# Retention and two expert layers on one core: one load task is moved ahead, one expert's row preparation is moved back

## The chip, the cores and the metric

One core of a Trainium2 chip runs the whole program. Times are microseconds of device time for one launch. The kernel before took 1059.43 us in the median of three runs (1049.46 to 1062.60). An execution of its own was profiled and is read below.

## The reference

Three stages, all in float32. The first is causal attention with a decay instead of a softmax; the second and third send each of 4608 tokens of 512 values through one of eight experts (512 to 1024 to 512, with a ReLU).

```python
scores = scale * q @ k.T                     # 8 x 8 heads, 576 x 576, width 64
x = (scores * gamma ** (i - j) * (j <= i)) @ v
x = x.transpose(0, 2, 1, 3).reshape(4608, 512)

logits = x @ w_gate                          # first layer: each token to its best expert
e = argmax(logits); out[t] = softmax(logits)[t, e] * (relu(x[t] @ w1[e]) @ w2[e])

logits = out @ w_gate2                       # second layer: all (token, expert) pairs by falling logit,
                                             # a token to the first expert that has room (576 each)
out2[t] = relu(out[t] @ w1b[e]) @ w2b[e]
```

In the second layer experts fill up one after the other; the kernel looks for them in eight phases, in the order in which they become full.

## The kernel before, in words

**Arithmetic.** Each f32 operand is split into two f16 parts, so a product is three f16 matmuls (high by high, high by low, low by high). Weights come in quarters of 512 KB through three `stage` buffers (`load_half`, L416 to L478): ACT writes the high part (L469), VectorE the low part (L472). The generator gives up control five times: the first turn issues loads 0 and 1, the next four each cast one quarter, the first two of these also issuing loads 2 and 3. Where `behind` is set, each load is pinned behind what SP was given before; casts are pinned likewise on their engines.

**First expert layer** (`moe1`, L988). Eight experts in order of their count, e = 0 to 7. `layer1` makes h for all of an expert's rows: 8 blocks of 24 matmuls into `ph`, which has two PSUM buffers; ACT takes the ReLU (L593), VectorE the rest (L594). `layer2` makes a tile of 128 rows with 24 matmuls of 512 columns; `out_rows` scales it and `second` (L1071) puts it to `X1`, by SP (L1077, the last tiles, 36 to 39 of 40) or by an indirect DMA of POOL (L1088). For e = 6 and e = 7 only `layer1` runs at first; their ten row tiles follow in `rest` (L1218), and the choice for the second layer begins under them.

Other work is hung on step numbers of `layer1`'s 192 matmuls. `prep(e)` (L1014) lists and gathers an expert's rows; each of its further turns normalises a tile of 128 rows (square L517, scaled copy L530, low half L533, all behind each other) and transposes it by DMA on SP (L544). Rows are built in three `xhl` buffers. For e = 6 these turns, which prepare the eighth expert (e = 7), stand at the steps in `N6`. `gate2` (L700) folds the second layer's gate into w2: four pairs of DMA transposes of w2 on SP (L711, two `w2T` buffer pairs) and sixteen small matmuls for each (L718, L719). For e = 6 its turns stand at `G6`: the first two issue pairs 0 and 1, the third uses pair 0 and issues pair 2, the fourth uses pair 1 and issues pair 3, the fifth uses pair 2; the last pair is used at step 24 of e = 7.

**Second expert layer** (`moe2`, L1744). `choose` finds the threshold at which the next expert is full, five rounds of a comparison on VectorE (L1545), a count on PE (L1551), and two small matmuls more (L1559, L1566); its "sum" (L1583) gives the expert's number, and `listed` its rows. All of it is issued piecewise by `during` (L1830): after each matmul the nominal time of its columns at 2.4 GHz is taken off three counters, and what has run out issues its next piece. `tasks` holds the loads and row turns to come, as pairs (first, function), one every 2700 ns (`GAP`) in the first phases. `prepare` (L1810) puts them there: for phase 0 the five turns of w1's `load_half` once the expert is known, for later phases everything once the list is known. `due(True)` runs tasks until none with `first` is left; `due(False)` runs all. w1's tasks and row turns have `first` set, w2's have not.

Phase 0 takes its rows from X1: three gathers before the last tiles are stored (`soon`, from the eighth row tile on), two behind them (`fetched`). PE transposes three of these tiles under the tenth row tile at its steps 12, 16 and 20 (`turned`: L550 on PE, L551 on ACT, L552 on VectorE), the other two at steps 76 and 88 of phase 0's `layer1`. Then `due(False)`, `fetched(0)` and `half(0, 2)` put w2's five tasks on the empty list, and phase 0 begins.

**Order.** PE's instructions, the loads, casts and row preparations named above are pinned to the program's order behind what precedes them on their engine. What is not pinned (the reads of PSUM, the scaling and storing of rows, the gathers) is placed in each engine's queue by a scheduler when the kernel is built. At run time each queue is worked in its order.

Of the kernel before, what the change touches and what calls it, by code (L numbers as in the profile page):

```python
# [36 lines left out]
RANK = (32, 40, 48)  # L37
N1 = (14, 82, 102, 122, 142, 170)
LOGITS = (96, 99, 101, 105, 109)
N6 = (24, 42, 60, 78, 94)  # L40
G6 = (4, 8, 40, 122, 139)
G7 = (30, 36, 70, 106, 140, 170)
R = 5
NONE = -1.0e30
# [658 lines left out]
def gate2(k, w, n):  # L703

    nc = k.nc
    pg = k.fps.tile([128, 8, 16], F32, name="tp")

    def turned(i):
        t = k.fp.tile([128, 2, 8, 128], F16, name="w2T", bufs=2)
        for z, x in enumerate((w.w2h, w.w2l)):  # L710
            pe(k, nc.sync.dma_start(t[:, z], x[:, 2 * i:2 * i + 2, :].rearrange("p f d -> p (f d)"), transpose=True))  # L711
        return t

    def used(i, t):
        for j in range(2):
            f = 2 * i + j
            for c in range(4):
                pe(k, nc.tensor.matmul(pg[:, f, :], t[:, 0, 4 * j + c, :], k.wgl[:, c, :], start=c == 0, stop=False, skip_group_check=True))  # L718
                pe(k, nc.tensor.matmul(pg[:, f, 0:8], t[:, 1, 4 * j + c, :], k.wgl[:, c, 0:8], start=False, stop=c == 3, skip_group_check=True))  # L719

    ts = [turned(0)]
    yield
    ts.append(turned(1))
    yield
    for i in range(4):
        used(i, ts[i])
        if i < 2:
            ts.append(turned(i + 2))
        if i < 3:
            yield  # L730
    f = k.fp.tile([128, 8, 8], F32, name="wgf", bufs=1)
    nc.vector.tensor_reduce(f, pg.rearrange("p s (n e) -> p s e n", n=2), op=OP.add, axis=AX.X)
    g = k.fp.tile([128, 8, 16], F16, name=f"wgh{n}", bufs=1)
    nc.vector.tensor_scalar(g[:, :, 0:8], f, 2.0 ** -7, None, op0=OP.mult)
    nc.vector.scalar_tensor_tensor(g[:, :, 8:16], f, 2.0 ** -7, g[:, :, 0:8], op0=OP.mult, op1=OP.subtract)
    return g
# [251 lines left out]
def moe1(k, X, X1, w1, w2):  # L988
# [110 lines left out]
    for e in range(8):  # L1099
# [24 lines left out]
        elif e < 7:  # L1124
            p1 = ahead
            for i in N6 if e == 6 else N1:
                steps[i] = lambda: next(p1, None)
# [25 lines left out]
        if e > 5:  # L1153
# [5 lines left out]
            gates[e] = gate2(k, w, e)  # L1159
            for i in G6 if e == 6 else G7:  # L1160
                steps[i] = partial(step, e, gates[e])
# [582 lines left out]
def moe2(k, X1, w1, w2, out, rest):  # L1744
# [9 lines left out]
    def side():  # L1754

        with k.tc.high_priority(offset=1000):
            t = next(aside[0], None)
        if t is None:
            aside.pop(0)
            prepare()  # L1760
        state.side = ASIDE.get(t, 0)
# [16 lines left out]
    def choose_on():  # L1778
        with k.tc.high_priority(offset=1000):
            state.left = next(choice, 1e9)  # L1780
        prepare()

    def half(n, i):

        w = weights.setdefault(n, K())
        g = load_half(k, w, (None, w1, w2)[i][ds(ev[n], 1)].rearrange("o d f -> (o d) f"), i, 4, behind=True)
        tasks.extend([(i == 1, lambda: next(g, None))] * 5)

    def soon():

        if 0 not in rows:
            rows[0] = [gather(k, X1[0:128 * (NS - LATE), :], lx[0][:, s:s + 1]) for s in range(SOON)]
            xTs[0] = new_xT(k)
# [16 lines left out]
    def prepare():  # L1810

        n = state.ph + 1
        if n == 0:
            if 0 in ev and 0 not in weights:
                half(0, 1)
        elif n in lx and n not in weights:
            half(n, 1)
            t = tasks[-5:]
            del tasks[-5:]
            r = [(True, partial(turned, n, s)) for s in range(5)]  # L1820
            pair = lambda *fs: (True, lambda: [f() for _, f in fs])
            tasks.extend([(True, partial(fetched, n))] + t[:2] + [pair(*r[:3])] + t[2:3] + [pair(*r[3:])] + t[3:])
            half(n, 2)

    def due(first):

        while tasks and (not first or any(x for x, _ in tasks)):
            tasks.pop(0)[1]()
# [46 lines left out]
    rest(resting)  # L1875
    while not lx:
        choose_on()
    due(False)
    soon()
    fetched(0)  # L1880
    for s in range(len(turns), SOON):
        turned(0, s)
    turns[:] = [partial(turned, 0, s) for s in range(SOON, 5)]
    half(0, 2)
    for ph in range(8):
        while ph and ph not in weights:
            if aside:
                side()
            else:
                choose_on()  # L1890
        due(True)
        state.ph = ph
        prepare()
        w = weights[ph]
        h = during(later(layer1(k, xTs[ph], w, CAP2, spans=None if ph else [[(0, 128 * SOON)], [(128 * SOON, CAP2 - 128 * SOON)]])))
        while not hasattr(w, "whole"):
            tasks.pop(0)[1]()
        for s in range(5) if ph < 7 else (4, 0, 1, 2, 3):
            tail = s == 4
            py = during(layer2(k, h, w, s, tail))  # L1900
            to_out(k, py, scales[ph][s], tail, out, out2)


def program(tc, q, kk, v, wg1, w11, w12, wg2, w21, w22, consts, out, dbg=None):
    nc = tc.nc
    ctx = ExitStack()
    k = K()
    k.pin = False
    setup(k, tc, nc, ctx, consts)
    moe_setup(k, ctx)  # L1910
    X = tc.dram_tile([128 * NT, W], F32, name="Xs")
    X1 = tc.dram_tile([128 * NS, W], F32, name="X1s")
    LG = tc.dram_tile([128 * NS, 8], F32, name="LGsd")
    k.wgl = split_gate(k, wg2, "wg2")
    select_setup(k)
    k.w = {0: K()}
    attention(k, q, kk, v, wg1, consts, X, [(load_half(k, k.w[0], w11[0], 1, 4, steps=False, spread=True), *CAST)], early(k, X))
    open_ffn(k)
    rest = moe1(k, X, X1, w11, w12)
    k.wn, k.xn, k.yn = 8, 9, 0  # L1920
    moe2(k, X1, w21, w22, out, rest)
    k.pin = False
    n = nc.values_load(k.again[0:1, 0:1], min_val=0, max_val=1, skip_runtime_bounds_check_because="0 or 1")
    with tc.For_i(0, n):
        overflow(k, X, X1, LG, w11, w12)
        anew(k, X1, w21, w22, out)
    if dbg:
        dbg(k, X, X1, LG)
    k.fctx.close()
    ctx.close()  # L1930
# [25 lines left out]
```

## Time and profile before

| | before |
|---|---|
| median of three runs | 1059.43 us |
| the three runs | 1049.46, 1059.43, 1062.60 us |
| the profiled execution | 1056.06 us |
| its span, first to last instruction | 1054.2 us |
| mean granted TensorE clock | 0.984 |
| PE, VectorE, ACT, POOL busy | 95%, 58%, 40%, 29% |

The profile shows instructions with their line, engine, operation and tiles. A wait is the idle time of an engine before an instruction, put down to what released it. PE is TensorE's matmuls; SPq and POOLq are the issues of DMAs. The granted clock is a share of 2.4 GHz, and 0.5 is the lower level of 1.2 GHz. In time, the first expert layer's seventh `layer1` runs from 503.94 us, the eighth from 540.5, the ten row tiles from 571 to 631, phase 0 of the second expert layer from 631.28.

### The profile page before, as it was taken

How to read it: one execution, taken by the hardware profiler on the slowest of the kernel's cores; microseconds unless marked ns; L12 is line 12 of the kernel's file. 1: busy time of each engine (PE TensorE's matmuls, PEld its weight loads, DVE VectorE, ACT ScalarE, POOL GpSimd, SP SyncE). 2: the span in 40 equal slices, each digit the busy share in tenths (PEclk: the TensorE clock that was granted, in tenths of full speed). 3: DMA queues.
4: the chain of work that ended last, by engine and by line, in shares of the span. 5: the costliest groups of instructions: out<-in, count | busy, mean ns of one | idle time of the engine just before them, and what ended most of it. 6: DMA issues, size and time to landing. Idle time of an engine off the chain costs nothing.

```text
span 1054.2 us, 23316 instructions
## 1 busy us (share of the span) xinstructions
PE 1003.0 (95%) x9165; PEld 669.1 (63%) x9165; DVE 611.6 (58%) x1648; ACT 426.5 (40%) x810; POOL 307.0 (29%) x542
## 2 busy tenths in 40 slices
PE   6999998889999999999899998999999999999995
PEld 5888887546665757474567445574747474757572
DVE  3556765786766657567443676575648484625230
ACT  2555644464546555455421244233324242323330
POOL 5444454331130303020320231414141413414101
PEclk9999998899999999999999999999999999999998
DMA  9999998597787887779951153758265546746501
GB/s 191 213 238 243 227 241 220 140 249 175 206 227 155 215 183 203 174 199 235 218 87 32 41 158 111 189 170 201 101 126 170 151 140 162 230 128 178 141 27 43
DMA packets 304918, 177.64 MB, mean 169 GB/s; under 512 B 239136, under 2 KB 272416, under 8 KB 304800
## 3 DMA queue, kind: packets, MB, share of 16 engines
q1 hardware_dynamic: 293680, 140.83, 57.7%
q0 software_dynamic: 11120, 35.24, 10.4%
q8 instruction: 74, 1.21, 0.5%
q14 instruction: 44, 0.36, 0.1%
HBM read 116.83 MB, written 31.02 MB: 140 GB/s over the span
## 4 chain that ended last, share of the span: by engine, by line
PE 75%; DMA 9%; DVE 8%; issue 3%; ACT 3%; SPq 1%; POOL 0%; POOLq 0%; ACTq 0%; DVEq 0%
PE py L614 29%; PE ph L588 27%; PE tp L123 7%; PE pO L123 4%; PE pS L123 4%; DMA xg<-Xs,ix 3%; DMA q<-in_q_dram 2%; PE py L610 2%; DMA xT<-xhl 2%; DVE w1l L472 1%; DVE hl L594 1%; DVE w2l L472 1%; DMA stage<-in_moe_w_dram 1%; SPq L123 1%; DVE xhl L533 1%
## 5 line engine op out<-in xcount | busy, mean ns | idle before, releaser
L588 PE MATMUL ph<-xT,w1h 128*128 128x288 f16 (+6 forms) x2048 | 357.4, 290 | 16.7 <-DVE hl L594 6.9
L588 PEld LDWEIGHTS <-w1h 128*128 128x128 f16 x2048 | 196.2, 98 | 77.3 <-issue 21.4
L588 PE MATMUL ph<-xT,w1l 128*128 128x288 f16 (+6 forms) x1024 | 225.9, 290 | 0.0
L614 PE MATMUL py<-w2l,hh 128*128 128x512 f16 x512 | 194.1, 379 | 1.0 <-DVE w2l L472 1.0
L614 PE MATMUL py<-w2h,hh 128*128 128x512 f16 x512 | 194.2, 379 | 0.3 <-ACT w2h L469 0.3
L614 PE MATMUL py<-w2h,hl 128*128 128x512 f16 x512 | 194.2, 379 | 0.0
L614 PEld LDWEIGHTS <-hh 128*128 128x128 f16 x1024 | 98.3, 98 | 109.4 <-issue 1.0
L593 ACT ACTIVATE hh<-ph 128x576 f16<-128x576 f32 (+6 forms) x136 | 80.8, 594 | 169.8 <-PE ph L588 168.2
L594 DVE SCALAR_TENSOR_TENSOR hl<-ph,hh 128x576 f16<-128x576 f32 (+6 forms) x136 | 93.9, 691 | 57.9 <-ACT hh L593 57.3
L588 PEld LDWEIGHTS <-w1l 128*128 128x128 f16 x1024 | 99.9, 98 | 29.0 <-issue 2.6
L472 DVE SCALAR_TENSOR_TENSOR w1l<-stage,w1h 128x1024 f16<-128x1024 f32 x60 | 73.1, 1222 | 41.6 <-ACT w1h L469 40.8
L614 PEld LDWEIGHTS <-hl 128*128 128x128 f16 x512 | 50.0, 98 | 57.0 <-issue 1.3
L472 DVE SCALAR_TENSOR_TENSOR w2l<-stage,w2h 128x1024 f16<-128x1024 f32 x64 | 78.2, 1223 | 11.6 <-ACT w2h L469 11.1
L503 POOL DMA_INDIRECT xg<-X1s,ix x40 | 46.1, 1152 | 108.3 <-DVE ix L658 56.7
L123 DVE TENSOR_TENSOR s<-pS,ct 128x512 f32<-128x512 f32 x72 | 46.4, 686 | 43.2 <-PE pS L123 43.1
L469 ACT ACTIVATE w2h<-stage 128x1024 f16<-128x1024 f32 x64 | 66.9, 1048 | 4.8 <-DMA stage<-in_moe_w_dram 4.8
L469 ACT ACTIVATE w1h<-stage 128x1024 f16<-128x1024 f32 x60 | 62.3, 1047 | 1.6 <-DMA stage<-in_moe_w_dram 1.6
L517 ACT ACTIVATE x1r<-py 128x512 bf16<-128x512 f32 x37 | 22.1, 596 | 96.2 <-PE py L614 64.3
L123 POOL TENSOR_TENSOR xTl<-xT,xTh 128x512 f16<-128x512 f32 x34 | 39.6, 1164 | 64.3 <-ACT xTh L123 64.2
L671 POOL TENSOR_TENSOR x1r<-nm,sc 128x1 f32<-128x1 f32 x34 | 6.4, 190 | 177.2 <-DVE nm L384 174.8
L123 ACT ACTIVATE kT<-tp 128x512 f32<-128x512 f32 x36 | 21.5, 597 | 87.4 <-PE tp L123 87.4
L503 POOL DMA_INDIRECT xg<-Xs,ix x36 | 42.3, 1176 | 43.4 <-DVE ix L658 29.2
(399 smaller groups left out, 1459.8 us busy)
## 6 DMA issues: line engine op xcount, KB each, us to landing
stage<-in_moe_w_dram SPq DMA_DIRECT2D x128, 512.0 KB, 4.6
X1s<-x1r SPq DMA_DIRECT2D x32, 257.0 KB, 3.2
k<-in_k_dram SPq DMA_DIRECT2D x32, 256.0 KB, 5.5
q<-in_q_dram SPq DMA_DIRECT2D x32, 256.0 KB, 5.5
v<-in_v_dram SPq DMA_DIRECT2D x32, 256.0 KB, 5.2
Xs<-xr SPq DMA_DIRECT2D x5, 1028.0 KB, 7.2
Xs<-xr POOLq DMA_DIRECT2D x3, 771.0 KB, 4.4
Xs<-xr POOLq DMA_DIRECT2D x1, 1028.0 KB, 5.6
```

The source lines that it names most:

```text
L123: return lambda *args, **kw: self.tc.keep_in_program_order(f(*args, **kw))
L469: d = nc.scalar.activation(at(h, i), t, AF.Copy, scale=128.0)
L472: d = nc.vector.scalar_tensor_tensor(at(l, i), t, 128.0, at(h, i), op0=OP.mult, op1=OP.subtract)
L503: nc.gpsimd.indirect_dma_start(out=xg[:M], out_offset=None, in_=src, in_offset=bass.IndirectOffsetOnAxis(ap=gidx[:M], axis=0))
L517: d = nc.scalar.activation(q.bitcast(mybir.dt.bfloat16), x, AF.Square, accum_out=sc[:, 0:1])
L533: nc.vector.scalar_tensor_tensor(h[:, 512:1024], x, sc[:, 1:2], h[:, 0:512], op0=OP.mult, op1=OP.subtract)
L588: pe(k, nc.tensor.matmul(ph[:, z, :b], x[:, c, F], xT[:, y + c, a:a + b], start=i == 0, stop=i == 11))
L593: nc.scalar.activation(oh, src, AF.Relu)
L594: nc.vector.scalar_tensor_tensor(ol, src, 0.0, oh, op0=OP.max, op1=OP.subtract)
L610: pe(k, nc.tensor.matmul(py[64 * z:64 * z + 64, 0:256], x[:, f, S], y[:, f, 256 * z:256 * z + 256], start=i == 0, stop=i == 23))
L614: pe(k, nc.tensor.matmul(py, x[:, f, S], y[:, f, :], start=i == 0, stop=i == 23))
L671: nc.gpsimd.tensor_tensor(xr[:, 512:513], n[:, 2:3], sc[:, 0:1], op=OP.mult)
```

## The change

Four edits. The steps in `N6` go from 24 to 94 to 46 to 126; the last three in `G6` go from 40, 122 and 139 to 137, 150 and 170. For phase 0, `prepare` puts w2's five tasks behind w1's as soon as the expert is known, and the call of `half(0, 2)` at the end of the row tiles is gone. `due` ahead of phase 0 runs only as long as a task with `first` is left.

```diff
-N6 = (24, 42, 60, 78, 94)
-G6 = (4, 8, 40, 122, 139)
+N6 = (46, 66, 86, 106, 126)
+G6 = (4, 8, 137, 150, 170)
@@ prepare()
         if n == 0:
             if 0 in ev and 0 not in weights:
                 half(0, 1)
+                half(0, 2)
@@ between rest(resting) and phase 0
-    due(False)
+    due(True)
     soon()
     fetched(0)
     for s in range(len(turns), SOON):
         turned(0, s)
     turns[:] = [partial(turned, 0, s) for s in range(SOON, 5)]
-    half(0, 2)
```

## Rows read from the trace of the kernel before

**Rows 1.** page part 1, busy time of each engine

```profile
PE 1003.0 (95%) x9165; PEld 669.1 (63%) x9165; DVE 611.6 (58%) x1648; ACT 426.5 (40%) x810; POOL 307.0 (29%) x542
```

**Rows 2.** waits of PE, 498 to 545 us: total, times, longest

```profile
PE ph L588 <- DVE sc L534: 3.7, 1, 3.7
PE ph L588 <- DVE hl L594: 2.8, 2, 1.6
```

**Rows 3.** timeline of PE: start, us, engine, line, instructions, [idle before]

```profile
503.94 0.43 PE L588 MATMUL ph<-xT,w1h 128*128 128x320 f16 x2
...
528.57 0.69 PE L588 MATMUL ph<-xT,w1h 128*128 128x320 f16 x2 [3.69 <-DVE sc L534]
...
543.78 0.17 PE L718 MATMUL tp<-wg2s,w2T 128*128 128x16 f16 x1
...
544.19 0.70 PE L588 MATMUL ph<-xT,w1h 128*128 128x320 f16 x4
544.73 0.43 PE L588 MATMUL ph<-xT,w1l 128*128 128x320 f16 x2
```

**Rows 4.** windows: us, PE, PEld, DVE, ACT, POOL busy, PEclk, DMA

```profile
528.57:531.97 3.40, 3.40 (x28) 2.13 (x28) 3.23 (x16) 1.24 (x3) 2.01 (x2) 0.53 0.25 45
...
644.88:647.91 3.03, 3.03 (x11) 1.28 (x12) 2.10 (x6) 1.69 (x3) 1.99 (x8) 0.51 0.36 139
```

**Rows 5.** timeline of ACT in the seventh expert's first layer

```profile
512.26 0.63 ACT L517 ACTIVATE xhl<-xg 128x512 bf16<-128x512 f32 x1 [2.51 <-DMA xg<-Xs,ix]
...
521.99 0.63 ACT L517 ACTIVATE xhl<-xg 128x512 bf16<-128x512 f32 x1 [2.79 <-DMA xT<-xhl]
...
526.35 0.63 ACT L517 ACTIVATE xhl<-xg 128x512 bf16<-128x512 f32 x1 [2.45 <-DMA xT<-xhl]
```

**Rows 6.** timeline of SP in the same layer

```profile
514.48 2.28 SPq L544 DMA_TRANSPOSE xT<-xhl  x1
516.86 2.41 SPq L711 DMA_TRANSPOSE w2T<-w2h  x1
...
521.67 4.27 SPq L544 DMA_TRANSPOSE xT<-xhl  x3
```

**Rows 7.** DMA of tile w2T, 490 to 560 us, from issue to landing

```profile
DMA to landing us min/median/max: 3.1/3.3/5.9
```

**Rows 8.** DMA of tile stage, 600 to 700 us, from issue to landing

```profile
DMA to landing us min/median/max: 3.6/4.2/4.9
```

**Rows 9.** waits of PE, 626 to 664 us

```profile
PE ph L588 <- DVE hl L594: 2.6, 2, 2.5
```

**Rows 10.** timelines of ACT and VectorE, phase 0 of the second layer

```profile
640.49 1.06 ACT L469 ACTIVATE w2h<-stage 128x1024 f16<-128x1024 f32 x1 [1.80 <-DMA stage<-in_moe_w_dram]
...
641.58 2.50 DVE L472 SCALAR_TENSOR_TENSOR w2l<-stage,w2h 128x1024 f16<-128x1024 f32 x2 [1.29 <-ACT w2h L469]
```

**Rows 11.** timeline of SP around the last row stores

```profile
622.69 0.34 SPq L1077 DMA_DIRECT2D X1s<-x1r  x1
...
635.03 0.32 SPq L1077 DMA_DIRECT2D X1s<-x1r  x1
635.56 1.54 SPq L438 DMA_DIRECT2D stage<-in_moe_w_dram  x3
```

**Rows 12.** waits of SP, 600 to 650 us

```profile
SPq L1077 <- POOL x1r L671: 8.7, 2, 5.5
```

**Rows 13.** timeline of POOL under the row tiles

```profile
617.94 1.40 POOL L503 DMA_INDIRECT xg<-X1s,ix  x1 [2.64 <-DVE key L1541]
```

**Rows 14.** timelines of PE and VectorE under the row tiles

```profile
603.29 0.17 PE L1583 MATMUL tp<-s,one_h 128*128 128x8 f16 x1
...
626.54 0.31 PE L1551 MATMUL tp<-ch,cmp 128*128 128x64 f16 x5
...
624.05 0.23 DVE L1569 SCALAR_TENSOR_TENSOR thf<-fstep,bw,tp 128x16 f32<-128x16 f32 x1 [1.76 <-PE tp L1566]
...
624.32 0.85 DVE L1545 TENSOR_TENSOR cmp<-key,thf 128x640 f16<-128x640 f32 x1
```

## The prediction

> **What bounds the kernel now.** I read the page first: TensorE is busy for 1003.0 of 1054.2 us [rows 1]. So a change here pays only what it takes from the idle or half-speed time of PE. The diff touches two stretches: the first layer of the seventh expert (served seventh, e = 6, from 503.94 us) and the border between the two MoE layers (604 to 663 us). For each I asked for PE's waits, then for the timeline of the queue that released them.
>
> In the seventh expert's first layer PE waits 3.7 us once and 2.8 us in two pieces, both times for VectorE [rows 2]; the granted clock then reads 0.53 for 3.40 us, the 1.2 GHz level, after an idle 3.69 us [rows 3, 4]. VectorE is not the cause. ACT works its queue in order, and the squares of the eighth expert's rows (L517) stand in it ahead of the reads of PSUM (L593): the square at 512.26 waited 2.51 us for a gather, those at 521.99 and 526.35 waited 2.79 and 2.45 us for a transposed row to leave its buffer [rows 5]. SP shows why those were late: row 0's transpose at 514.48, then the gate's transposes of w2 (one of the two is shown), and only at 521.67 rows 1 to 3 [rows 6].
>
> At the border PE waits 2.6 us (2.5 and 0.2), again for VectorE [rows 9], and the next 3.03 us have a clock of 0.51 [rows 4]. Here it is the second weights of phase 0: ACT stands 1.80 us for their load, and VectorE's 2.50 us of two low halves (L472) lie ahead of the read that frees PSUM [rows 10]. The loads were issued at 635.56, behind the last row store at 635.03 [rows 11].
>
> **The change, part B (N6, G6): what it removes.** One step is a matmul of 320 columns: four take 0.54 us [rows 3], so 0.136 us. Rows were normalised at steps 24 to 94, now at 46 to 126. Squares of rows 3 and 4 now stand behind the reads of blocks 3 and 4 instead of ahead of block 3's; and with the gate's later turns at 137 and 150, no w2 transpose is left between the rows' transposes. Row 0's was in use from 514.48 to 521.99, 7.5 us; row 1's from 521.67 to 526.35, 4.7 us [rows 5, 6]. From an issue at about 512.5 row 0's buffer is free by 517 to 520. The third square's new place (step 106, PE at about 518.5) and the fourth's (step 126, about 522) then wait for less than the 1.5 us of slack that two PSUM buffers leave. Removed: 3.7 + 2.8 us of waits, and 3.40 us at 0.53, which is 1.6 less what is not matmul there; I take 1.5. Together 8.0 us. Least: the 3.7 and the 1.5 alone, 5.2.
>
> **Part B: what it adds.** No instruction is added. But the gate's third pair of w2 turns now goes out behind row 4's transpose. Row 4 is squared at about 522 and its transpose is out by 526 (row 3 now: squared at 521.99, out by 525.94 [rows 5, 6]). The second w2 transpose starts 1.3 to 2.4 us later [rows 6] and lands 3.3 us after that (3.1 to 5.9) [rows 7]: 530.6 to 531.7, I take 531.5. PE wants it at step 170: 503.94 + 170 x 0.136, plus two gate groups of 0.41 us and five logits groups half as long [rows 3], is 529.0. So PE waits 2.5 us at this new place; bounds 0 (row 4 is early) and 6.0 (landing 5.9 makes 4.5, the clock 1.5 more). I add no clock here, though the 2.5 us at the border were enough for 1.5 us of it [rows 4, 9]. The eighth expert's own first matmul, at about 534.5, finds row 4 landed. Part B: -8.0 + 2.5 = -5.5 us.
>
> **Part A (w2 of phase 0): where its five tasks now stand.** The list grows where the first choice's sum is done, 603.29, six matmuls into the eighth expert's first tile [rows 14]. A task runs every 2700 ns, 13 matmuls of 213 ns. Five tasks of w1, then w2: first two loads behind the 23rd matmul of the third tile (before that tile's own store is issued, behind the second's), first casts on ACT and VectorE behind the 12th of the fourth, the next two at the first and 14th of the fifth, the last cast four matmuls into phase 0. due(True) leaves that last one there.
>
> What holds SP: the second tile's store went only at 622.69. SP waited 5.5 us for POOL's scale of that row (L671) alone [rows 11, 12], and POOL had three gathers ahead of it, the first from 617.94 [rows 13]. The diff does not touch that order. So the loads go out at 622.69 + 0.53 (the distance in [rows 11]) = 623.2, 12 us earlier than now, and land 4.2 us later (3.6 to 4.9) [rows 8]: 627.4. The page "DMA: Bandwidth & Descriptors" of the Trainium skill (section "Anatomy of one DMA") gives 2.0 us plus bytes at 436 GB/s, an estimate of 3.2 us for 512 KB; by it the wait below is 1 us shorter, and the landings here do not show it.
>
> What stands behind the cast: the queues' order is written at build time, and the scheduler took loads as landed too early in the very same pattern now (1.80 us on ACT, [rows 10]). I take it that it puts the first cast on ACT ahead of the fourth tile's square and its low half on VectorE ahead of the choice's next threshold (624.05) [rows 14]. Then VectorE is blocked until 627.4 + 1.06 + 1.25 = 629.8; threshold and comparison took 1.12 us from 624.05 [rows 14]: 630.9. PE's count matmul, now at 626.54, waits **4.4 us** (3.8 to 5.1 by the landings; 0 if the queues are ordered the other way). Behind it ACT and VectorE hold two more casts (1.06 and 1.25 each) ahead of the PSUM copies of phase 0's row turns, which have two buffers: between 0 and 3.3, I take 1.7. A wait over 2.4 us was followed by the 1.2 GHz level both times [rows 3, 4, 9]: 1.5 more. The last cast lies ahead of phase 0's first PSUM read: 0 to 1.2, 0.5. Paid: 8.1 us (0 to 11.1).
>
> What comes back: 2.6 us of waits and half of 3.03 us, 1.5: 4.1 us [rows 4, 9]. Part A: +8.1 - 4.1 = +4.0 us.
>
> **Sum.** -5.5 + 4.0 = -1.5 us. The profiled execution took 1056.06 us (1.9 outside its span), so 1054.5. The median of the three runs is 3.4 higher, their spread 13.1; the forecast lies 4.9 under that median.
>
> **The rivals.** (1) *Both parts pay.* The cast is queued behind the comparison, or the store goes early, so nothing is paid at the border: -5.5 - 4.1 = -9.6, 1046.5. For it: 12 us of earlier issue. Against: [rows 12, 13]. The same page's section "Rules for kernel authors" would have it so: issue the DMA early, compute, wait late. No run here shows it; only half of the rule is met, as the wait comes early too. (2) *The same, and w2's turns land in time*: -8.0 - 4.1 = -12.1, 1044. For it: landings of 3.1 us [rows 7]. Against: they queue behind row 4. (3) *Slower*: the loads land later than 5.7 us after their issue. Gains are 8.0 - 2.5 + 4.1 = 9.6, the price 8.1 at a landing of 4.2; each further us is PE's. At 8.5 us it is +2.8, 1059. For it: gathers of rows run beside these loads, and a transpose took 5.9 [rows 7]. Against: no stage load did over 4.9 [rows 8].
>
> **How the numbers follow.** Forecast 0.45 (alone 1050 to 1058), rival 1 0.25, rival 2 0.1, rival 3 0.2. The range takes all four and the spread of single runs: 1043 to 1063. Two per cent, about what a measurement of this kernel tells from no change, is 21 us; no case reaches it, so same 0.93, faster 0.04, slower 0.03 for orders that shift elsewhere when the queues are laid out anew.
>
> **What would show it.** Right for B: no PE wait over 1 us before step 137 of that layer, clock 1.00 throughout, one wait of 2 to 3 us at the third gate group. Right for A: phase 0's w2 loads at about 623 less B's gain, ACT idle before the first cast, a PE wait of 4 to 5 us before a count matmul in the eighth expert's fourth or fifth tile, and none behind phase 0's fourth block. Wrong: ACT's first cast without idle (rival 1), POOL's scale ahead of the gathers, or PE waiting for the row turns of the eighth expert.

## The result and the profile after

The changed kernel is slower: 1061.8 us against 1055.0 us of before (medians of 20 runs each), a ratio of 1.0062 with a 95% interval of 1.0039 to 1.0085. That is +6.5 us (4.1 to 9.0), where the forecast was -1.5. The profiled execution took 1062.01 us.

The page (part 1) shows that PE's own work did not change, as [rows 1] of before has 1003.0 us; the loss is waiting and half speed:

```profile
span 1060.2 us, 23317 instructions
...
PE 1004.3 (95%) x9165; PEld 668.9 (63%) x9165; DVE 612.8 (58%) x1648; ACT 426.4 (40%) x810; POOL 305.0 (29%) x542
```

**The border between the layers.** PE's waits, 626 to 664 us (total, times, longest), which answer to [rows 9]:

```profile
PE tp L1551 <- DVE nm L382: 5.8, 1, 5.8
PE ph L588 <- DVE hl L594: 1.4, 2, 1.2
```

The old wait has shrunk from 2.6 to 1.4 us, and a new one of 5.8 us stands in the row tiles, at the count matmul. The timeline of SP shows the loads early, at 623.23 instead of 635.56 [rows 11]:

```profile
622.61 0.34 SPq L1077 DMA_DIRECT2D X1s<-x1r  x1
623.23 1.35 SPq L438 DMA_DIRECT2D stage<-in_moe_w_dram  x2
626.20 0.34 SPq L1077 DMA_DIRECT2D X1s<-x1r  x1
626.74 0.37 SPq L438 DMA_DIRECT2D stage<-in_moe_w_dram  x1
634.42 0.34 SPq L1077 DMA_DIRECT2D X1s<-x1r  x1
```

and those of ACT and VectorE (start, us, [idle before and who ended it]) show that their consumers were earlier still:

```profile
620.60 0.69 ACT L669 ACTIVATE x1r<-py,nm 128x512 f16<-128x512 f32 x1 [1.01 <-DVE nm L383]
629.15 1.06 ACT L469 ACTIVATE w2h<-stage 128x1024 f16<-128x1024 f32 x1 [7.87 <-DMA stage<-in_moe_w_dram]
...
630.24 1.23 DVE L472 SCALAR_TENSOR_TENSOR w2l<-stage,w2h 128x1024 f16<-128x1024 f32 x1 [7.92 <-ACT w2h L469]
631.38 0.23 DVE L1569 SCALAR_TENSOR_TENSOR thf<-fstep,bw,tp 128x16 f32<-128x16 f32 x1
631.53 0.15 DVE L1571 TENSOR_TENSOR lof<-bw,tp 128x1 f32<-128x1 f32 x1
631.64 0.82 DVE L1545 TENSOR_TENSOR cmp<-key,thf 128x640 f16<-128x640 f32 x1
```

Both engines stood for 7.9 us at the first cast, each with work behind it that PE needed: the threshold L1569 ran at 631.38, in before at 624.05 [rows 14]. PE resumed at 632.52, and the window behind that (us, PE, PEld, DVE, ACT, POOL busy, PEclk, DMA) shows the 1.2 GHz level for 5.58 us, worth 2.8 us:

```profile
632.52:638.10 5.58, 5.58 (x31) 3.09 (x31) 4.14 (x9) 3.77 (x5) 0.19 (x1) 0.50 0.45 111
```

**The seventh expert's first layer.** PE's waits, 498 to 545 us, which answer to [rows 2]; then ACT's one wait for a transposed row, where [rows 5] has two, and the issue of that row on SP, where [rows 6] has 514.48 and 2.28 us:

```profile
PE ph L588 <- DVE sc L382: 4.3, 1, 4.3
PE tp L719 <- DMA w2T<-w2l: 2.1, 1, 2.1
PE tp L693 <- DMA x1T<-x1r: 2.0, 1, 2.0
```

```profile
507.81 7.67 SPq L544 DMA_TRANSPOSE xT<-xhl  x1
...
521.36 0.63 ACT L517 ACTIVATE xhl<-xg 128x512 bf16<-128x512 f32 x1 [5.90 <-DMA xT<-xhl]
```

The rows' squares did move, and the wait on the row buffer moved with them, in one piece of 5.90 us instead of 2.79 and 2.45. The forecast had it gone. The half-speed stretch came with it (window behind the 4.3 us, 526 to 532 us; columns as above):

```profile
526.00:532.00 6.00, 5.12 (x34) 3.08 (x34) 4.65 (x20) 2.26 (x3) 2.05 (x2) 0.50 0.48 88
```

The 2.0 us at L693 are a wait for transposed output rows of the sixth expert, which SP issued at 499.65 and 502.27, ahead of the first moved row. The forecast has no term for it; it is 1.7 us in a second profile of this kernel, and what brings it stays open.

### The profile page after: what moved, and what is told of

Same layout as the page of the kernel before. It is cut to its first block, busy times and chain, and to the rows that moved or that the text cites. A ratio compares the mean times of both kernels' runs of the same rounds, so it can differ in the third digit from the quotient of the medians.

```text
span 1060.2 us, 23317 instructions
## 1 busy us (share of the span) xinstructions
PE 1004.3 (95%) x9165; PEld 668.9 (63%) x9165; DVE 612.8 (58%) x1648; ACT 426.4 (40%) x810; POOL 305.0 (29%) x542
## 4 chain that ended last, share of the span: by engine, by line
PE 73%; DMA 9%; DVE 8%; issue 3%; ACT 3%; SPq 2%; POOL 1%; POOLq 0%; ACTq 0%; DVEq 0%
PE py L614 28%; PE ph L588 28%; PE tp L123 6%; PE pO L123 3%; PE pS L123 3%; PE py L610 2%; DMA xg<-Xs,ix 2%; DMA q<-in_q_dram 2%; SPq L123 2%; DVE w2l L472 1%; DMA xT<-xhl 1%; DMA v<-in_v_dram 1%; DVE hl L594 1%; DMA stage<-in_moe_w_dram 1%; DMA X1s<-x1r,to 1%
## 5 line engine op out<-in xcount | busy, mean ns | idle before, releaser
L614 PE MATMUL py<-w2l,hh 128*128 128x512 f16 x512 | 194.1, 379 | 1.1 <-DVE w2l L472 1.1
L614 PE MATMUL py<-w2h,hh 128*128 128x512 f16 x512 | 194.2, 379 | 0.2 <-ACT w2h L469 0.2
L614 PE MATMUL py<-w2h,hl 128*128 128x512 f16 x512 | 194.2, 379 | 0.0
L614 PEld LDWEIGHTS <-hh 128*128 128x128 f16 x1024 | 98.3, 98 | 109.4 <-issue 0.9
L594 DVE SCALAR_TENSOR_TENSOR hl<-ph,hh 128x576 f16<-128x576 f32 (+6 forms) x136 | 93.7, 689 | 65.4 <-ACT hh L593 64.7
L614 PEld LDWEIGHTS <-hl 128*128 128x128 f16 x512 | 50.0, 98 | 57.1 <-issue 1.4
```

Of the source, the lines that this page charges most:

```text
L594: nc.vector.scalar_tensor_tensor(ol, src, 0.0, oh, op0=OP.max, op1=OP.subtract)
L614: pe(k, nc.tensor.matmul(py, x[:, f, S], y[:, f, :], start=i == 0, stop=i == 23))
```

## The experiments

The table has three stretches of each profiled execution, between starts of instructions on PE's timeline: the first layers of the seventh and eighth expert (first matmul of 320 columns to the first one of the second layer, L614), from the first choice's sum (L1583) to phase 0's first matmul, and phase 0's first layer. The last column is the timed ratio to before. The first stretch differs by up to 4.3 us between kernels that are the same there (before, a_only, a_pool and a_late_casts: 67.20 to 71.53), so for it the ratios decide; the other two repeat within 0.7 us, save for phase 0's layer where its loads are as in before (30.30 to 31.97).

| kernel | first layers | sum to phase 0 | phase 0's layer | ratio, 95% interval |
|---|---|---|---|---|
| before | 67.20 | 27.99 | 31.28 | 1 |
| after | 71.88 | 36.57 | 28.69 | 1.0062 [1.0039, 1.0085] |
| after2 | 69.38 | 36.54 | 28.69 | one run, 1061.09 us |
| a_only | 68.39 | 37.07 | 28.70 | 1.0074 [1.0046, 1.0102] |
| b_only | 69.00 | 27.98 | 31.97 | 1.0018 [0.9997, 1.0040] |
| n6_only | 65.79 | 28.00 | 31.59 | 0.9982 [0.9958, 1.0006] |
| g6_only | 67.83 | 27.99 | 30.30 | 0.9987 [0.9962, 1.0012] |
| a_pool | 69.59 | 34.94 | 29.88 | 1.0049 [1.0026, 1.0072] |
| a_late_casts | 71.53 | 27.98 | 30.78 | 0.9980 [0.9959, 1.0002] |
| buf5 | 61.17 | 28.27 | 31.92 | 0.9946 [0.9926, 0.9965] |
| b_buf5 | 63.58 | 28.62 | 30.49 | 0.9967 [0.9948, 0.9987] |
| n6_buf5 | 62.31 | 28.62 | 31.58 | 0.9959 [0.9931, 0.9986] |
| g6_buf5 | 65.17 | 28.27 | 31.87 | 0.9961 [0.9931, 0.9991] |
| b_loads_late | 65.68 | 28.11 | 31.57 | 0.9983 [0.9961, 1.0006] |
| late3_buf5 | 60.69 | 28.27 | 28.69 | 0.9922 [0.9892, 0.9952] |

### Each part alone

a_only has the diff's lines in `prepare`, `due` and `half(0, 2)` with the old N6 and G6; b_only the new N6 and G6 alone; n6_only and g6_only one of these two.

> Only the loads and casts of phase 0's second weights are moved (N6 and G6 as before). Theory 1, the border owns the loss: a PE wait of 4 to 6 us before a count matmul in the row tiles, 8 to 9 us more from the first choice's sum to phase 0, 2.6 us less in phase 0's first layer: 6 us slower than before (ratio 1.0057). Theory 2, the loss is shared with the row preparation: about 2 us slower, as the cast's wait varies with the landing. In the seventh expert's first layer the trace should be that of before.

> Only N6 and G6 are changed. My prediction gave -5.5 us. Theory 1 (the landings of 13 us in the changed kernel's profile belong to that one execution, since they begin before the first moved instruction): landings of 4 to 9 us, one PE wait of 2 to 3 us for the gate's turn, -4 to -6 us. Theory 2 (the new order itself makes the landings long, or its waits for row buffers, gate turns and logits rows are there anyway): 8 us of PE waits again and 0 to +5 us.

> Only the row steps are moved, the gate turns stay at 40, 122 and 139. If the moved rows are what helps, -3 to -6 us; if the gate's transposes ahead of the rows' are what holds the row buffers, the two ACT waits for row buffers stay and the gain is under 2 us. No PE wait for a gate turn in either case.

> Only the gate turns are moved, rows stay at 24 to 94. If the gate's transposes hold the row buffers, ACT's waits for them shrink from 5.2 to under 2 us and PE's 3.7 us wait goes; a wait of 2 us for the gate's third turn comes: -1 to -4 us. If rows are late for the gathers alone: 0 to +2 us.

Part A alone costs 7.8 us (4.9 to 10.8), so it carries the whole loss. PE's waits of a_only, 626 to 668 us:

```profile
PE tp L1551 <- DVE nm L382: 6.7, 1, 6.7
PE ph L588 <- DVE hl L594: 1.4, 2, 1.2
```

Part B alone is +1.9 us (-0.3 to 4.2), not -5.5. The waits of b_only, 498 to 545 us, hold both halves of the answer: ACT still waits for a transposed row and PE behind it, and the gate's wait is 3.9 us:

```profile
ACT xhl L517 <- DMA xT<-xhl: 4.5, 1, 4.5
...
PE ph L588 <- DVE sc L382: 3.8, 2, 2.9
PE tp L718 <- DMA w2T<-w2h: 2.7, 1, 2.7
PE tp L719 <- DMA w2T<-w2l: 1.2, 1, 1.2
```

With the rows alone or the turns alone ACT's wait for the transposed row is 5.6 and 5.3 us, and both intervals hold 1. g6_only has no w2 transpose between the rows' any more, and the wait is there all the same: it doesn't take these transposes to hold the row buffer.

### Two cures for part A

a_pool is part A, and POOL issues the three gathers of `soon()` behind the scale of the row that is to be stored:

```diff
-    nc.gpsimd.tensor_tensor(xr[:, 512:513], n[:, 2:3], sc[:, 0:1], op=OP.mult)
+    k.scaled = nc.gpsimd.tensor_tensor(xr[:, 512:513], n[:, 2:3], sc[:, 0:1], op=OP.mult)
...
-            rows[0] = [gather(k, X1[0:128 * (NS - LATE), :], lx[0][:, s:s + 1]) for s in range(SOON)]
+            with k.tc.issue_after(k.scaled.ins): rows[0] = [gather(k, X1[0:128 * (NS - LATE), :], lx[0][:, s:s + 1]) for s in range(SOON)]
```

a_late_casts issues the two first loads early, as part A does, and has the four casts in phase 0, as before has them (`half` returns its five tasks here):

```diff
-                half(0, 1)
+                tasks.extend(half(0, 1))
+                casts[:] = half(0, 2)
+                tasks.append(casts.pop())
...
-    half(0, 2)
+    tasks.extend(casts)
```

> Part A alone, and POOL is told to issue the three row gathers of phase 0 behind the scale of the row being stored (L671), so that the store, and the loads behind it on SP, no longer wait for the gathers. Theory: part A loses because its first cast is queued ahead of work of the choice while its load, held behind that store, lands too late. Then the loads go out at about 617 instead of 623, land before ACT and VectorE reach the first cast, PE's wait for the count matmul L1551 falls from 6.7 us (part A alone) to under 1 us, nothing waits at phase 0's border, and the time is about 4 us under that of before (ratio 0.996); some 11 us under part A alone. Rival: what costs is where the casts stand and the traffic of four loads beside the gathers, wherever the loads start; then the time stays at 1.005 or above.

> The other cure for part A: only the first two loads of phase 0's second weights are issued early (at the place part A has them), their casts stay in phase 0 where the kernel before has them. Theory: an early load costs nothing if nothing that waits for it is queued early: no wait over 1 us at L1551 in the row tiles, the first cast on ACT runs without idle (1.80 us before), PE's waits at phase 0's fifth block (2.6 us) and the half-speed stretch behind them go, and the time is 2 to 4 us under before (ratio 0.996 to 0.998). Rival: the third and fourth load, which still go out behind the last store, now make their casts wait instead, and the gain is given back: ratio 1.000. Second rival (traffic of the early loads delays gathers or stores): over 1.002.

a_pool's store and first two loads went out early as meant, at 617.00 and 617.94. But two of its casts show where the wait went (ACT's timeline), and PE's longest wait, 626 to 668 us, stands behind the later of them:

```profile
622.80 1.06 ACT L469 ACTIVATE w2h<-stage 128x1024 f16<-128x1024 f32 x1 [1.62 <-DMA stage<-in_moe_w_dram]
...
633.09 1.06 ACT L469 ACTIVATE w2h<-stage 128x1024 f16<-128x1024 f32 x1 [4.51 <-DMA stage<-in_moe_w_dram]
```

```profile
PE tp L550 <- DVE c L1563: 4.9, 1, 4.9
```

The first cast's wait fell from 8.6 us (a_only) to 1.62. The third load goes out at 627.24 only, behind the next store (626.70), which POOL again held, waiting 3.69 us for a gathered row; the third cast, queued ahead of the row turns' copies, waits 4.51 us, and PE 4.9 at L550. The theory's -4 us was a miss, and its rival's 1.005 came: the loss is still 5.2 us (2.8 to 7.6). The block passes to the next cast as long as casts stand in the row tiles.

a_late_casts has no such wait: 27.98 us from the sum to phase 0, as before, so two early loads and their traffic cost nothing there. Against before it is -2.1 us (-4.3 to 0.2, so not clear of nothing), and its third cast gives something back, waiting 3.79 us for a load that still left behind the last store (ACT's timeline in phase 0):

```profile
637.84 1.05 ACT L469 ACTIVATE w2h<-stage 128x1024 f16<-128x1024 f32 x1
...
644.38 1.06 ACT L469 ACTIVATE w2h<-stage 128x1024 f16<-128x1024 f32 x1 [3.79 <-DMA stage<-in_moe_w_dram]
```

### The row buffers of part B

buf5 is before with buffers of their own for the eighth expert's rows 3 and 4 (two tiles that lie idle until later); the others add it to part B or to one half of it.

```diff
+own = lambda k, i: (k.fp.tile([128, 8, 128], F16, name=("ovhh", "ovhl")[i], bufs=1).rearrange("p a b -> p (a b)"), k.fp.tile([128, 6], F32, name="sc", bufs=12))
-            x, sc = normalise(k, rows[e][s], not e, pin=True)
+            x, sc = normalise(k, rows[e][s], not e, own(k, s - 3) if e == 7 and s > 2 else None, pin=True)
```

> The kernel before, with row buffers of their own for the eighth expert's last two rows, so that no square (L517) waits for a transpose to leave its buffer. Steps and gate turns are those of before. Theory (the buffer wait is what PE's waits in the seventh expert's first layer come from): ACT's waits of 2.79 and 2.45 us for the transposes vanish, with them PE's 2.8 us behind L594 and most of the 3.7 us and the half-speed stretch behind it: 3 to 6 us less, ratio 0.994 to 0.997. Rival: the transposes themselves are late (the DMA rings are full in that stretch), so the squares go early but the transposed w2 of the gate or the eighth expert's first matmul waits instead: ratio 0.999 to 1.001.

> Part B alone (rows and gate turns moved) with row buffers of their own for the eighth expert's last two rows. Theory (part B doesn't pay because the row buffer wait moves with the rows): ACT has no wait on a transpose, PE no wait behind it, and only the gate's wait for the third pair of w2 turns (2 to 4 us) is left: 4 to 6 us less than before, ratio 0.994 to 0.996. Rival: the transposes of rows 1 to 4 and then those of w2 are late by themselves, so PE waits as long at the gate turn as it waited at the reads: ratio 0.999 to 1.002, as part B alone (1.0018).

buf5 is 5.7 us faster than before (3.7 to 7.8). All waits of PE in its seventh expert's first layer, 498 to 545 us, are 1.5 us, where [rows 2] has 6.5 (and a_only, a_pool and a_late_casts, which are as before there, 5.0, 7.4 and 8.9):

```profile
PE ph L588 <- DVE sc L382: 1.2, 2, 0.8
PE ph L588 <- DVE sc L383: 0.3, 1, 0.3
```

So the forecast named the right cause of those waits, the squares held by a row buffer. Being rid of it is worth 5.7 us, nearer the forecast's least (5.2) than its 8.0. It was wrong that part B is rid of it. With part B on top, the same stretch of b_buf5 has the gate's wait of 3.1 us, and the gain is 3.5 us (1.4 to 5.5):

```profile
PE tp L718 <- DMA w2T<-w2h: 1.6, 1, 1.6
PE tp L719 <- DMA w2T<-w2l: 1.5, 1, 1.5
PE ph L588 <- DVE sc L382: 1.0, 1, 1.0
```

> Of part B only the later rows, the gate turns as before, with row buffers of their own for the eighth expert's last two rows. Theory (with the buffers the rows' place costs nothing, what part B then loses against the buffers alone is the gate's turns behind row 4): as the buffers alone, ratio 0.993 to 0.996, no wait of PE for w2T over 1 us in the seventh expert's first layer. Rival: the later rows themselves hold up the reads of PSUM or the eighth expert's first matmul: 0.996 to 0.999.

> Of part B only the later gate turns, the rows as before, with row buffers of their own for the eighth expert's last two rows. Theory (the gate's wait for w2T is what part B pays): the rows' transposes go out earlier than in part B, those of w2 right behind them, so the wait for w2T is 0 to 2 us and the ratio lies between those of the buffers alone (0.9946) and of part B with buffers (0.9967). If the wait is 3 us as with part B, the ratio is 0.997; if it is 0, the later rows, not the later turns, make the wait.

Neither half gains anything beside the buffers. All four intervals overlap, so the 2 us between buf5 and b_buf5 are not clear of noise, and which half would cost them is not settled: n6_buf5 has no wait on w2T, as expected, but a wait of 1.4 us for row 4 itself and 1.6 us for x1T; g6_buf5 waits 1.0 us for w2T and 2.9 us at one block of the layer.

### The changed kernel again, and what holds row 0's transpose

after2 is the changed kernel unchanged.

> The kernel after once more, for a second profile. If its structure is what the first profile shows, PE again waits 5 to 7 us at the count matmul L1551 of the eighth expert's fourth tile, and phase 0 begins 35 to 38 us behind the first choice's sum; and in the seventh expert ACT waits once for a transposed row (4 to 6 us) and PE for the gate's w2T (2 to 3 us). If the landings of 13 to 14 us of the row transposes in the first profile were one execution's, they are 6 to 9 us here.

The structure repeats: 5.7 us at L1551, 36.54 us from the sum to phase 0, 6.1 us of ACT for the transposed row, 2.1 us for w2T. Row 0's transpose again holds SP for 5.90 us at its issue and is out of its buffer 12.7 us after it (508.71 to 521.38), so its late landing is no accident of one execution.

b_loads_late is part B alone with later steps for the loads and casts of the eighth expert's second weights:

```diff
-        for i in (2, 34, 50, 66, 82) if e == 0 else range(13, 190, 30) if e == 5 else (16, 64, 112, 160):
+        for i in (2, 34, 50, 66, 82) if e == 0 else range(13, 190, 30) if e == 5 else (100, 120, 140, 160) if e == 6 else (16, 64, 112, 160):
```

> Part B alone, with the third and fourth load of the eighth expert's second weights (512 KB each, issued at 501.67 and 508.37 in part B alone) moved behind the steps in which the rows are transposed. Theory (the DMA engines are full, so row 0's transpose lands when the bytes ahead of it are through): some 2 us earlier for each load that is no longer ahead, so row 0's buffer is free at 517 to 519 instead of 521.6, ACT's wait for it falls from 4.5 to 0 to 2.5 us, and the time is 1 to 3 us under part B alone (ratio 0.997 to 1.000). Rival: the transposes of the tile rows and the gathers, which remain, set the landing: 521 to 522 as before, a wait of 4 to 6 us, ratio 1.001 to 1.003.

ACT's wait for a transposed row is gone (the fourth square, at 521.71, has no idle ahead of it), and so is PE's behind it; what is left is the gate's, which the forecast put at 2.5 (0 to 6.0). PE's waits of b_loads_late, 495 to 545 us:

```profile
PE tp L718 <- DMA w2T<-w2h: 2.8, 1, 2.8
PE tp L719 <- DMA w2T<-w2l: 1.1, 1, 1.1
PE ph L588 <- DVE sc L382: 1.0, 1, 1.0
```

It is -1.8 us against before (-4.1 to 0.6) and 3.7 us less than b_only by the two ratios, whose intervals just overlap. The expectation had two loads moved. In the trace it is one (512 KB): the fourth goes out 17.3 us after the layer's start instead of 6.4, while the third stands ahead of that start in both. Row 0 is issued 9.5 us after the layer's start in both, but the issue holds SP for 1.90 us instead of 3.87 (SP of b_only, then of b_loads_late):

```profile
511.43 3.87 SPq L544 DMA_TRANSPOSE xT<-xhl  x1
515.19 1.90 SPq L544 DMA_TRANSPOSE xT<-xhl  x1
```

and its buffer is free at most 6.5 us later (521.71 less 515.19) instead of 10.2. Two casts on ACT and VectorE moved along with the load; this run alone doesn't part the two.

The bytes do. These are windows from the layer's start to the square that takes row 0's buffer, of before, after, b_only, n6_only and b_loads_late in this order (us, PE, PEld, DVE, ACT, POOL busy, PEclk, DMA share, GB/s; a share over 1 means that packets' times overlap):

```profile
503.94:521.99 18.05, 15.28 (x144) 11.13 (x143) 9.57 (x24) 9.15 (x18) 6.75 (x13) 1.00 1.13 223
499.30:521.36 22.06, 20.10 (x191) 14.61 (x190) 10.62 (x25) 10.08 (x18) 6.86 (x13) 1.00 1.13 186
501.97:521.58 19.61, 18.70 (x171) 13.61 (x170) 10.43 (x25) 9.84 (x18) 7.53 (x13) 1.00 1.12 206
506.59:527.28 20.69, 20.29 (x207) 14.95 (x206) 10.43 (x25) 9.84 (x18) 8.26 (x14) 1.00 1.09 217
505.69:521.71 16.02, 15.06 (x132) 10.89 (x131) 8.14 (x23) 8.90 (x17) 4.66 (x11) 1.00 1.08 218
```

Time by rate is 4.0, 4.1 and 4.0 MB in the first three, and 4.0 to 4.1 in after2, a_only, g6_only, a_pool and a_late_casts as well, whether the time was 18.05 us or 22.06, and with row 0's issue anywhere from 7.7 to 10.5 us behind the layer's start. n6_only, where a pair of w2 transposes (0.5 MB) goes out ahead of row 0's, has 4.5; b_loads_late, with one load (0.5 MB) less ahead, 3.5 at most. So, by one execution of each run, what had to move first set when the row buffer came free, as the theory had it, and part B takes none of it away.

### Both cures together

late3_buf5 has the buffers, three of phase 0's second loads early, the fourth behind the first cast, and all casts in phase 0.

```diff
-    for i in range(3 if spread else 2):
+    for i in range(first or (3 if spread else 2)):
...
-        if i < 2:
-            load(i + 2)
+        if len(stages) < 4:
+            load(len(stages))
```

> Both cures together: the eighth expert's last two rows have buffers of their own, and of phase 0's second weights three loads are issued early, the fourth behind the first cast, all casts stay in phase 0. Theory: the gain of the buffers (0.9946) and that of late casts behind early loads add up, and with the third load early too the cast that waited 3.79 us for its load in the run with two early loads no longer does: about 2 to 4 us under the run with the buffers alone, 1048 to 1051 us at a before of 1057 (ratio 0.991 to 0.993). Rival: the waits of PE at the border are not the loads but VectorE's low halves (1.22 us each, two of them ahead of a read of PSUM), so nothing is gained beside the buffers: ratio 0.994 to 0.996.

It is faster than before by 8.3 us (5.1 to 11.4), at 1049.09 us. From buf5 alone its ratio is not clear (the intervals overlap); what it gains beyond that is read from the trace. Its layer in the seventh expert and its border (windows: us, PE, PEld, DVE, ACT, POOL busy, PEclk, DMA) have PE at work for 58.82 of 60 us, the granted clock at the 2.4 GHz level throughout, and the wait behind L594 is the 1.4 us of after:

```profile
502.00:562.00 60.00, 58.82 (x632) 43.67 (x631) 28.50 (x79) 22.03 (x37) 13.10 (x19) 1.00 0.76 135
594.00:652.00 58.00, 56.15 (x422) 32.56 (x421) 43.45 (x140) 24.54 (x47) 13.36 (x33) 1.00 0.40 123
```

Phase 0's layer took the 28.69 us of after, where buf5 has 31.92, and the stretch ahead of it none of after's 8.6 us.

## Why the prediction was wrong

**Where it broke.** The sum had part B at -5.5 and part A at +4.0 us. Timed alone, B is +1.9 and A +7.8; both steps erred in the same direction, B by some 7 us, A by some 4. (The two add up to 9.7 where both together measure 6.5; the intervals leave room for that, and no run splits it further.)

**Part B, the step that failed.** "From an issue at about 512.5 row 0's buffer is free by 517 to 520", and with that the removal of 8.0 us. The time in use was taken from row 1 (4.7 us) and row 0 (7.5 us), as a length that begins with the issue, and as if what stood between the rows on SP, the transposes of w2, were what made it long. In after, with no w2 transpose between, row 0 was issued at 507.81 and its buffer was free at 521.36, 13.5 us later; in b_only it was 511.43 to 521.58, 10.2 us. Nor was the 7.5 us a good measure of the old order: in a_only, a_pool and a_late_casts, which have it too, the same row took 11.0, 11.5 and 12.0 us. What holds still is the amount moved, 4.0 to 4.1 MB since the layer's start, 18 to 22 us of the DMA engines' work; an earlier issue doesn't shorten it and moved squares still wait for it. The rows [rows 6] held a warning: issues of 2.28 to 2.41 us where others take 1.3 (1.29 at 530.10 in after) tell that SP could not get its transposes taken. The prediction's own sign of being wrong, PE waiting for the row turns of the eighth expert, came: the 4.3 us of after stand behind their scale (L382).

**Part B, what held.** That the squares on ACT held up the reads of PSUM was right, and freeing them is worth 5.7 us by buf5. The 1.5 us of slack, given without its rows, fits: 5.9 us of ACT's wait became 4.3 of PE's in after, 4.5 became 2.9 in b_only. The gate's wait for the third pair was right in place, and 2.1 us in after and after2, 3.9 in b_only, against 2.5.

**Part A, mechanism right, terms too small.** Loads at 623.23 (forecast 623.2 less B's gain), behind the store that POOL's gathers hold; first cast ahead of the choice's threshold on both queues; a wait at the count matmul: all as forecast. The wait was 5.8 us, not 4.4, as the load landed 5.9 us after its issue and not 4.2 (its cast began at 629.15). The half-speed stretch behind it was 5.58 us, worth 2.8 us where 1.5 stood. The 1.7 us for two more casts ahead of the row turns' copies were not seen. Together the stretch to phase 0 grew by 8.6 us in after, against 7.6. The return was 2.6 us (31.28 to 28.69), against 3.6. That makes +6.0 in the profile, and 4.9 to 10.8 timed.

**Its sums.** Two are slightly off. With the other terms as taken, a landing of 5.9 us makes the gate's wait 5.1, not 4.5; and 627.4 + 1.06 + 1.25 is 629.7, not 629.8. Neither changes the forecast by more than 0.1 us. The page "DMA: Bandwidth & Descriptors" of the Trainium skill (section "Anatomy of one DMA") gives its 2.0 us plus bytes at 436 GB/s for DMAs that POOL issues. These loads go out on SP, so the 3.2 us are no estimate of them, and the sum did not use them.

**The rivals.** Rivals 1 and 2 had nothing paid at the border; they fell with the first cast's idle of 7.87 us. The rule they leaned on, of the Trainium skill's page "DMA: Bandwidth & Descriptors" (section "Rules for kernel authors"), issue early and wait late, is borne out by late3_buf5, which keeps both halves of it: there phase 0's layer is 3.2 us shorter than in buf5 and the stretch ahead of it no longer. Rival 3 had its condition met, 5.9 us over the 5.7 at which it decided, but by its own working that makes +0.2 and not +6.5: it priced the landing and kept the 8.0 us of part B. What was missing among the rivals is the one that came: the row buffer's wait stays, wherever the rows stand, for the bytes ahead of it stay.

**The range and the chances.** The range reached to 1063 and holds 1061.8, and the time is within 2% as forecast; but the likeliest case had the sign wrong, and the range, widened for the spread of single runs, held the result by luck.

## What to carry to other kernels

An early load is worth something only if what waits for it is not queued early as well: on an engine that works in order, a cast that stands ahead of its load's landing stops everything behind it, here 7.9 us on two engines. Before moving work away from a late transfer, ask why that transfer is late; if the DMA engines are full, another order gives the same wait to another instruction, and a buffer more, or a load less ahead of it, is the cure. Count the bytes that have to move before it, over several executions, rather than the time from one issue to its landing. An issue on SP that takes two or three times its usual time is a row that can tell this beforehand.

## What the runs showed of the hardware

An issue of a DMA transpose on SP took 1.24 us at 501.92 in b_only, and the first one behind the eighth expert's fourth weight load took 3.87 us there, 5.90 in after2 and 7.67 in after; the instructions behind it on SP wait as long. The transpose that was issued so in after landed 13.5 us after its issue began. Its landing followed the bytes and not the issue: 4.0 to 4.1 MB since the layer's start in eight runs, in 18.05 to 22.06 us. And what the clock did behind a wait of PE differed: it stood at the 1.2 GHz level for 5.58 us behind 5.8 us of waiting at the border of after and for 3.40 us behind 3.7 in before [rows 3, 4], but not at all behind the 2.9 us that ended at 527.11 in b_only (columns as above):

```profile
527.11:533.92 6.81, 4.09 (x42) 2.84 (x42) 4.59 (x19) 2.96 (x4) 1.36 (x2) 1.00 0.57 104
```
